# The last 512 positions of a down projection, by pairs of tiles and partly by seven products for eight

## The chip, the cores and the metric

The kernel runs on one core of a Trainium2 chip. The metric is the device time of one execution in microseconds. Before the change the median of three timed runs is 467.15 us (467.04 to 467.17).

A core has five engines that run side by side and meet at semaphores: TensorE (PE; its weight loads are listed apart as PEld), VectorE (DVE), ScalarE (ACT), GpSimd (POOL) and SyncE (SP), from which all DMA transfers of this kernel are issued, one after the other.

## The reference

A layer norm over 2048 positions of 512 channels feeds two branches. Branch A is a windowed attention (32 heads, 8 keys each, every second position) with its output weights `wo`. Branch B is two layers with a squared ReLU, then a Silu. The result is the input plus their product.

```python
def _B_ref(x, w1, b1, w2, b2):                 # D = 512, F = 1792
    h = jnp.einsum("bsd,df->bsf", x, w1) + b1
    r = jnp.where(h > 0, h, 0)
    h = r * r
    return jnp.einsum("bsf,fd->bsd", h, w2) + b2

x = A_x                                        # 1 x 2048 x 512
xn = _layernorm(x, axis=-1)
s = _A_ref(xn, A_wqkv, A_wo)                   # attention, then o @ wo
g = _silu(_B_ref(xn, B_w1, B_b1, B_w2, B_b2))
return x + s * g
```

What the change touches is the second einsum, the down projection, for the last quarter of the positions.

## The kernel before

All matrix products are in float32 precision, made of three passes each: an operand is split into a high part that TensorE takes as float32r and a low rest, and a product is high x high, high x low and low x high (`PASSES`). A split costs a copy on ACT and a subtraction on VectorE or GpSimd. The query, key, value and up projections already replace eight products of blocks by seven in large parts, with sums and differences of blocks as operands; the down projection does not.

The down projection is tiled into chunks of `C` = 512 positions (`NCH` = 4), each of four tiles of 128 positions (`TPC` = 4). It runs over `NF` = 14 blocks f of 128 of the 1792 inner channels. `down(c, f, j)` gives three matmuls of 512 columns into the bank `pbs[c, j]`, with 128 positions of `h` standing in the array and the rows of w2 moving. `begin` writes the bias b2 into a bank before; `gate` takes Silu out of it afterwards. The four banks have the tag "acc", of which there are four.

`h` is made from the up projection's result `u`, which for chunks 2 and 3 is loaded from the memory `su` by `load_ut`, six blocks ahead, into a ring of 12 pieces of 2 KB per partition (the tag "z" of the pool `keep`). `make_h`, two blocks ahead, squares it on ACT (with a ReLU first for half of the blocks), once into the high part and once in place, and an E instruction takes the difference as low part. Two blocks share a buffer of the tag "h", of which there are two.

Beside this, VectorE works through the attention in eight units of 256 positions. Its results are stored to `so`, loaded by `load_o` in another order, transposed by `trans_o` on VectorE, split (ACT, then `lowo`), and multiplied by `wo` in `out_product`: 12 matmuls of 512 columns a tile. `finish` multiplies this by the gate, adds x and stores the tile. In chunk 3 the out products of tiles 8 and 9 stand ahead of its first block, those of 10 and 11 after f = 5 and f = 6, those of 12 and 13 before the last three blocks; then each tile does its last three blocks and its gate, and the out products of tiles 14 and 15 end the kernel, the last one in two halves of 256 columns.

The order of work on each engine is not that of the program. `Book` records every instruction, plans the whole kernel by prices and due times, and then fixes the order on each engine. Only TensorE keeps the program's order. Instructions given to `E` go to VectorE or GpSimd, as the plan chooses. Every instruction is issued by one helper, so all have the same line in the profile (L163), and the names of tiles tell them apart: `pb` is a bank of the down projection, `pw` of an out product, `ut` and `h` its inputs, `z` a gated tile, `v`, `pv`, `Lp` are attention, `oq`, `oTf`, `oT` its outputs on the way to the out product, `pv` on TensorE a bank of the value projection.

Of the kernel before, what the change touches and what calls it, by code (L numbers as in the profile page):

```python
# [55 lines left out]
HOME2 = (Q0, T2, T3, K1, T4, V0, V1)  # L56

CUT = (Q0, T2, T3, T4, V1)

WARM = 20  # L60
WARM2 = 1
# [505 lines left out]
def trace(ctx: ExitStack, tc: tile.TileContext, plan, x, wqkv, wo, w1, b1, w2, b2, out):  # L567
# [37 lines left out]
    def split(hi, lo, src, eng):  # L605
        high(hi, lo, src)
        low(hi, lo, src, eng)
# [252 lines left out]
    def load_w2(f):  # L860
        w2raws[f] = piece(f"w2r{f}")
        dma(w2raws[f], w2[f * P:(f + 1) * P, :])
# [637 lines left out]
    def load_ut(c, f):  # L1500
        uts[c, f] = keep.tile([P, 2, 256], F32, name=f"ut{c}_{f}", tag="z", bufs=12)
        n = 256 * (c % 2)
        dma(uts[c, f], su[f][:, :, n:n + 256])

    def make_h(c, f):
        if (c, f) == (0, 0):
            h = hs[c, f] = [wts.tile([P, 512], FR, name=f"h{c}_{f}_{i}", tag=f"s{i}") for i in (T4, V1)]
        else:
            if f % 2 == 0 or (c, f) == (0, 1):
                hpair[f // 2] = p2.tile([P, 2, 2, 512], FR, name=f"h{c}_{f}", tag="h", bufs=2)  # L1510
            h = hs[c, f] = [hpair[f // 2][:, f % 2, i] for i in range(2)]
        n = 256 * (c % 2)
        if c >= NCH // 2:
            parts = [(uts.pop((c, f)).rearrange("p e n -> p (e n)"), h)]
        elif f < 4:
            parts = [(u0[f, e][:, n:n + 256], [x[:, e * 256:(e + 1) * 256] for x in h]) for e in range(2)]
        else:
            parts = [(u0[f // 2][f % 2][:, :, n:n + 256], [x.rearrange("p (e n) -> p e n", e=2) for x in h])]
        for u, (hi, lo) in parts:
            if f % 2:  # L1520
                A.activation(u, u, AF.Relu)
            A.activation(hi, u, AF.Square)
            A.activation(u, u, AF.Square)
            E.tensor_sub(lo, u, hi.bitcast(F32))
# [14 lines left out]
    def begin(c, j):  # L1539

        pbs[c, j] = psA(f"pb{c}_{j}")
        A.activation(pbs[c, j], b2t, AF.Copy)

    def down(c, f, j):
        h, w, n = hs[c, f], w2s[f], (j % 2) * 256 + j // 2 * P
        for k, (a, b) in enumerate(PASSES):
            PE.matmul(pbs[c, j], h[a][:, n:n + P], w(f % 2, b), start=False, stop=f == NF - 1 and k == 2,
                      skip_group_check=True)

    oqs, oTs = {}, {}  # L1550

    def load_o(u):
# [40 lines left out]
    def finish(t, eng, xt=None, cols=slice(0, D)):  # L1593
        z = gs[t // TPC, t % TPC]
        if xt is None:
            xt = xrs.pop(t)
        V.tensor_mul(z[:, cols], z[:, cols], pws[t][:, cols])
        eng.tensor_add(z[:, cols], z[:, cols], xt[:, cols])
        dma(tile_rows(out, t)[:, cols], z[:, cols])
# [10 lines left out]
    def split_wo(i):  # L1610
        for g in range(2):
            split(wot[:, 0, 2 * i + g], wot[:, 1, 2 * i + g], rwo[i][:, g], E)

    sequence = [(c, f) for c in range(NCH) for f in range(NF)]

    def ahead_h(c, f):
        i = c * NF + f
        if i + 6 < len(sequence) and i + 6 >= NCH // 2 * NF:
            load_ut(*sequence[i + 6])
        if i + 2 < len(sequence):  # L1620
            make_h(*sequence[i + 2])

    for j in range(TPC):
        begin(0, j)
    make_h(0, 1)
    for c in range(NCH):
        last = c == NCH - 1
        t0 = c * TPC
        for f in range(NF):
            if c == 0 and f in (2, 3):  # L1630
                load_wo(f - 2)
            if c == 0 and f < 8:
                load_w2(f + 6)
                split_w2(f + 6)
            if c == 0 and f in (5, 7):
                split_wo((f - 5) // 2)
            if c:
                if f < 2:
                    finish(t0 - 4 + f, E)
                if f == 2:  # L1640
                    load_o(c * 2 - 1)
                    load_r(t0 - 2)
                    load_r(t0 - 1)
                elif f == 4:
                    trans_o(t0 - 2)
                    trans_o(t0 - 1)
                elif f == 5:
                    lowo(t0 - 2)
                    lowo(t0 - 1)
                elif f == 6:  # L1650
                    out_product(t0 - 2, psT(f"pw{t0 - 2}"))
                elif f == 7:
                    finish(t0 - 2, E)
                    out_product(t0 - 1, psT(f"pw{t0 - 1}"))
                elif f == 8:
                    finish(t0 - 1, E)
            if f >= 7:
                load_o(c * 2)
            if f in (9, 10) and not last:
                load_r(t0 + f - 9)  # L1660
            if f == 11:
                for i in range(2):
                    trans_o(t0 + i)
            if f == 12:
                for i in range(2):
                    lowo(t0 + i)
                load_o(c * 2 + 1)
            ahead_h(c, f)
            if f == 0 and c == 0:
                pass  # L1670
            elif c == 0 and f == 1:
                for i in range(2):
                    for j in range(TPC):
                        down(c, i, j)
            elif f < (NF - 3 if last else NF - 2):
                for j in range(TPC):
                    down(c, f, j)
        if not last:
            for j in range(TPC):
                for i in (2, 1):  # L1680
                    down(c, NF - i, j)
                gate(c, j)
                begin(c + 1, j)
            for i in range(2):
                out_product(t0 + i, psT(f"pw{t0 + i}"))
        else:
            for i in range(2):
                out_product(t0 + i, psT(f"pw{t0 + i}"))
            for i in range(2, TPC):
                trans_o(t0 + i)  # L1690
            for i in range(2, TPC):
                lowo(t0 + i)
            xl = []
            for h in range(2):
                t = four(f"xlast{h}", [2, 512])
                r0 = t0 * P + h * UP
                dma(t.rearrange("p e n -> p (e n)"), x[r0:r0 + UP, :].rearrange("(p e) n -> p (e n)", e=2))
                xl += [t[:, e] for e in range(2)]
            for j in range(TPC):
                for f in range(NF - 3, NF):  # L1700
                    down(c, f, j)
                gate(c, j)
                if j < 2:
                    finish(t0 + j, V, xl[j])
            for j in range(2, TPC):
                n = D // 2 if j == TPC - 1 else D
                for i in range(0, D, n):
                    cols = slice(i, i + n)
                    out_product(t0 + j, (psL if i else psT)(f"pw{t0 + j}_{i}"), cols)
                    finish(t0 + j, V, xl[j], cols)  # L1710

    return book.arrange()

# [21 lines left out]
```

## Time and profile before

| what | value |
|---|---|
| median of three timed runs | 467.15 us |
| the profiled execution | 466.68 us |
| its span | 464.9 us |
| TensorE busy | 458.6 us (99%) |
| VectorE busy | 411.0 us (88%) |
| ScalarE busy | 309.9 us (67%) |
| GpSimd busy | 296.7 us (64%) |
| granted clock of TensorE | 1.0 |

The span goes from the first to the last instruction that the profiler recorded; the time of an execution holds a little more. A group of instructions is listed with its names (out<-in), its shapes, its count, the summed time, the mean duration of one, and the idle time ahead of it with what ended that. Matmuls overlap in the pipeline, so that the mean duration of one (some 390 ns) is longer than its pace; the pace is read from the chain or from start times. Some matmul records are missing from the trace.

### The profile page before, as it was taken

The numbers are of one execution on the slowest core, as the hardware profiler recorded it, in microseconds if no ns is written. First come the engines' busy times: TensorE is split into PE (matmuls) and PEld (weight loads), VectorE is DVE, ScalarE is ACT, GpSimd is POOL, SyncE is SP. The second block draws the span as 40 slices with busy tenths as digits, with TensorE's granted clock in tenths as the row PEclk, the third lists the DMA queues.
The fourth block names the chain that finished last, engine by engine and source line by source line (L and its number), as shares of the span: only waits on it lengthen the run. The fifth ranks groups of instructions, "written<-read, shape, count | busy, mean of one in ns | idle before, by whom it ended". The sixth has DMA issues, their size and how long they took to land.

```text
span 464.9 us, 6411 instructions
## 1 busy us (share of the span) xinstructions
PE 458.6 (99%) x2109; PEld 380.9 (82%) x2109; DVE 411.0 (88%) x349; ACT 309.9 (67%) x589; POOL 296.7 (64%) x309
## 2 busy tenths in 40 slices
PE   8999999999999999999999999999999999999996
PEld 5788888888888888888888888888888888888885
DVE  5984579989999999999999999998999999999432
ACT  5757889956664748477585798796449635953440
POOL 2286438745999899956461699786636655556440
PEclk9999999999999999999999999999999999999999
DMA  7799889899987997475264488597665697541302
GB/s 275 218 249 260 258 260 243 201 299 266 234 230 243 236 274 211 149 208 130 69 170 108 135 254 199 133 256 243 164 154 134 198 229 205 158 139 43 115 0 91
DMA packets 72589, 88.83 MB, mean 191 GB/s; under 512 B 6764, under 2 KB 52076, under 8 KB 72556
## 3 DMA queue, kind: packets, MB, share of 16 engines
q1 hardware_dynamic: 72556, 88.43, 69.9%
q8 instruction: 16, 0.26, 0.2%
q14 instruction: 17, 0.14, 0.1%
HBM read 54.80 MB, written 30.47 MB: 183 GB/s over the span
## 4 chain that ended last, share of the span: by engine, by line
PE 96%; DMA 1%; DVE 1%; ACT 0%; SPq 0%; issue 0%
PE pb L163 33%; PE uX L163 16%; PE pm L163 12%; PE pw L163 9%; PE uZ L163 8%; PE pq L163 8%; PE pv L163 4%; PE uY L163 4%; DMA wqraw<-in_A_wqkv 1%; SPq L163 0%; DVE wq L163 0%; PE pxT L163 0%; DVE z L163 0%; ACT wq L163 0%; DVE st L163 0%
## 5 line engine op out<-in xcount | busy, mean ns | idle before, releaser
L163 PE MATMUL pb<-w,h 128*128 128x512 f32 x592 | 149.2, 390 | 0.0
L163 PEld LDWEIGHTS pb<-w,h 128*128 128x128 f32 x592 | 110.9, 188 | 23.5 <-POOL h L163 0.4
L163 DVE TENSOR_TENSOR pr<-k,qp 128x2048 f32<-128x2048 f32 x32 | 72.8, 2274 | 2.4 <-ACT qp L163 1.8
L163 DVE TENSOR_TENSOR pv<-v,Lp 128x2048 f32<-128x2048 f32 x32 | 73.0, 2283 | 0.7
L163 DVE TENSOR_REDUCE v<-pv 128x256 f32<-128x2048 f32 x32 | 72.9, 2279 | 0.5
L163 DVE TENSOR_REDUCE L<-pr 128x128 f32<-128x2048 f32 x32 | 72.8, 2276 | 0.4
L163 POOL TENSOR_TENSOR h<-ut,h 128x512 fp32r<-128x512 f32 x25 | 32.2, 1301 | 28.6 <-ACT ut L163 28.6
L163 PE MATMUL pw<-wot,oT 128*128 128x512 f32 (+1 forms) x204 | 45.5, 377 | 0.0
L163 POOL TENSOR_TENSOR h<-u,h 128x256 fp32r<-128x256 f32 (+1 forms) x30 | 30.6, 1035 | 22.8 <-ACT u L163 21.2
L163 PEld LDWEIGHTS pw<-wot,oT 128*128 128x128 f32 x204 | 36.8, 188 | 7.1
L163 ACT ACTIVATE h<-ut 128x512 fp32r<-128x512 f32 x28 | 16.4, 627 | 21.9 <-PE pb L163 12.2
L163 ACT ACTIVATE ut<-ut 128x512 f32<-128x512 f32 x42 | 24.7, 626 | 9.3 <-DMA ut<-su 9.3
L163 POOL TENSOR_TENSOR u<-u,more 128x512 f32<-128x512 f32 x14 | 18.1, 1301 | 19.6 <-ACT more L163 19.2
L163 ACT ACTIVATE u<-uX,b1t 128x512 f32<-128x512 f32 x28 | 19.2, 684 | 15.5 <-PE uX L163 15.3
L163 POOL TENSOR_TENSOR oT<-oTf,oT 128x512 fp32r<-128x512 f32 x16 | 25.5, 1601 | 3.3 <-ACT oT L163 3.3
L163 ACT ACTIVATE u<-u 128x512 f32<-128x512 f32 (+1 forms) x54 | 26.1, 527 | 0.1
L163 ACT ACTIVATE oT<-oTf 128x512 fp32r<-128x512 f32 x16 | 18.2, 1139 | 11.5 <-DVE oTf L163 6.7
L163 ACT ACTIVATE h<-u 128x512 fp32r<-128x512 f32 (+1 forms) x36 | 17.5, 529 | 10.5 <-PE pb L163 10.4
L163 DVE TENSOR_TENSOR z<-z,pw 128x512 f32<-128x512 f32 (+1 forms) x17 | 11.1, 650 | 12.2 <-ACT z L163 7.3
L163 ACT ACTIVATE stg<-pm 128x512 f32<-128x512 f32 x30 | 17.7, 599 | 5.8 <-PE pm L163 5.6
L163 PE MATMUL pq<-wq,XA 128*128 128x512 f32 x78 | 20.2, 392 | 0.3 <-DVE wq L163 0.3
L163 PE MATMUL uZ<-SA,w1s 128*128 128x512 f32 x84 | 20.2, 390 | 0.0
(193 smaller groups left out, 1049.5 us busy)
## 6 DMA issues: line engine op xcount, KB each, us to landing
k<-sk SPq DMA_DIRECT2D x8, 960.0 KB, 7.6
v<-sv SPq DMA_DIRECT2D x8, 960.0 KB, 7.4
su<-u SPq DMA_DIRECT2D x28, 256.0 KB, 3.3
ut<-su SPq DMA_DIRECT2D x28, 256.0 KB, 3.8
x<-in_A_x SPq DMA_DIRECT2D x16, 256.0 KB, 4.6
sk<-stg SPq DMA_DIRECT2D x8, 512.0 KB, 4.0
sq<-stg SPq DMA_DIRECT2D x8, 512.0 KB, 3.7
sv<-stg SPq DMA_DIRECT2D x8, 512.0 KB, 3.5
```

What stands on the lines that cost most here:

```text
L163: ins = f(*a, **k)
```

## The change

Chunks 0 to 2 stay as they are. Chunk 3 is done by two pairs p of tiles (12 and 13, then 14 and 15), each in seven steps s. A step takes the blocks f = s and s + 7 for both tiles of the pair. Its operands are a 2 x 2 arrangement of blocks (two tiles, two f) against a 2 x 2 arrangement (two f, the left and right 256 columns of w2).

A plain step is 12 matmuls of 512 columns into banks 0 and 1. A step of seven (`SEVENTHS`: the last three of pair 0, the last five of pair 1) is seven products of three passes with 256 columns, spread over four banks, with sums of blocks as operands:

- `sum_w2`, during chunk 2, loads the two blocks of w2 again for s = 2 to 6, forms four sums of 256 columns, and splits them.
- `make_step` makes, beside the squares of a plain step, four sums of 128 columns of `h` and splits these too. The buffers come from the tag "h", or, for one step at a time, from the attention's "v" (`place_h`; `fill` makes steps as far as buffers allow).
- `join` copies the four banks of a pair out and adds their quarters up with seven additions, then takes Silu.

The out products of tiles 8 to 13 move between the steps (`jobs`); those of 14 and 15 follow the last `join`.

```diff
+DSEVEN = range(2, 7)
+SEVENTHS = range(4, 7), DSEVEN
+WHOME = {2: "m", 3: "m", 4: f"b{T1}", 5: f"b{K0}", 6: f"b{Q1}"}
...
+    def sum_w2(s):
+        for f in (s, s + NF // 2):
+            load_w2(f)
+        a, b = (w2raws.pop(f) for f in (s, s + NF // 2))
+        lo, hi = slice(0, 256), slice(256, 512)
+        E.tensor_sub(a[:, lo], a[:, hi], a[:, lo])
+        E.tensor_sub(a[:, hi], b[:, hi], a[:, hi])
+        E.tensor_sub(b[:, hi], b[:, hi], a[:, lo])
+        E.tensor_sub(b[:, lo], b[:, lo], b[:, hi])
...
+        for i, r in enumerate((a, b)):
+            split(t[i][:, 0], t[i][:, 1], r, E)
+        wsum[s] = t
...
+    def place_h(p, s):
+        if s in SEVENTHS[p]:
+            tag = "h" if live["v"] else "v"
+            live[tag].append((p, s))
+            if tag == "v":
+                return att.tile([P, 2, 7, P], FR, name=f"hs{p}_{s}", tag="v")
+            return p2.tile([P, 2, 7, P], FR, name=f"hs{p}_{s}", tag="h", bufs=2)
+        if s % 2 == 0:
+            cuts[p] = p2.tile([P, 2, 2, 4, P], FR, name=f"hs{p}_{s}", tag="h", bufs=2)
+            live["h"].append((p, s + 1))
+        return cuts[p][:, s % 2]
...
+    def make_step(p, s):
+        u = uts.pop((p, "s", s)).rearrange("p (q n) -> p q n", n=P)
...
+        A.activation(part, part, AF.Relu)
+        n = 3 if s in SEVENTHS[p] else 4
+        A.activation(h[:, 0, :n], u[:, :n], AF.Square)
+        A.activation(u, u, AF.Square)
+        E.tensor_sub(h[:, 1, :n], u[:, :n], h[:, 0, :n].bitcast(F32))
+        if s in SEVENTHS[p]:
+            f = piece(f"fs{p}_{s}").rearrange("p (q n) -> p q n", n=P)
+            E.tensor_add(f[:, 0], u[:, 3], u[:, 2])
+            E.tensor_sub(f[:, 1], f[:, 0], u[:, 0])
+            E.tensor_sub(f[:, 2], u[:, 0], u[:, 3])
+            E.tensor_sub(f[:, 3], u[:, 1], f[:, 1])
+            A.activation(h[:, 0, 3:], f, AF.Copy)
+            E.tensor_sub(h[:, 1, 3:], f, h[:, 0, 3:].bitcast(F32))
...
+    def begin_pair(p):
+        banks[p] = [psA(f"pd{p}_{i}") for i in range(4)]
+        for i in range(2):
+            A.activation(banks[p][i], b2t, AF.Copy)
+
+    def step(p, s):
...
+        for bank, half, q, r, cols in ((0, lo, 1, v[1], lo), (1, lo, 2, t[1], lo), (2, lo, 0, v[0], lo),
+                                       (3, lo, 3, t[0], lo), (3, hi, 5, t[0], hi), (2, hi, 4, t[1], hi),
+                                       (0, hi, 6, v[1], hi)):
+            for k, (a, c) in enumerate(PASSES):
+                PE.matmul(b[bank][:, half], h[:, a, q], r(c)[:, cols],
...
+    def join(p):
...
+        for t, b in zip((za, zb, x, y), banks.pop(p)):
+            A.activation(t, b, AF.Copy)
+        E.tensor_add(x[:, hi], x[:, hi], x[:, lo])
+        E.tensor_add(za, za, x)
+        E.tensor_add(za[:, hi], za[:, hi], y[:, lo])
+        E.tensor_add(x[:, hi], x[:, hi], y[:, hi])
+        E.tensor_add(zb[:, lo], zb[:, lo], x[:, hi])
+        E.tensor_add(x[:, hi], x[:, hi], y[:, lo])
+        E.tensor_add(zb[:, hi], zb[:, hi], x[:, hi])
+        for e, z in enumerate((za, zb)):
+            A.activation(z, z, AF.Silu)
+            gs[NCH - 1, 2 * p + e] = z
...
+            if c == NCH - 2 and f % 2 == 0 and f // 2 < len(DSEVEN):
+                sum_w2(DSEVEN[f // 2])
...
+    jobs = {(0, 0): [(leave, t0 - 4)], (0, 1): [(leave, t0 - 3), (oT_of, t0 // 2 - 1), (rows_of, t0 // 2 - 1)],
+            (0, 3): [(leave, t0 - 2)], (0, 5): [(leave, t0 - 1), (oT_of, t0 // 2), (rows_of, t0 // 2)],
+            (0, 6): [(join, 0), (leave, t0), (begin_pair, 1)],
+            (1, 3): [(leave, t0 + 1), (oT_of, t0 // 2 + 1), (rows_of, t0 // 2 + 1)],
+            (1, 6): [(join, 1)]}
+    for p in range(2):
+        for s in range(NF // 2):
+            i = n * NF + p * (NF // 2) + s
+            step(p, s)
+            if i + 6 < len(sequence):
+                load_step(sequence[i + 6][0], sequence[i + 6][2])
+            for f, a in jobs.get((p, s), ()):
+                f(a)
+            fill((p, s))
+    for t in range(t0 + 2, NT):
+        leave(t, True)
```

`leave` is the out product and the finish of a tile, `oT_of` the load, transposition and split of two tiles' attention outputs, `rows_of` the load of two tiles of x. `load_step` loads the `u` of a step in two transfers of 128 KB with runs of 512 bytes, where `load_ut` had one of 256 KB with runs of 1 KB.

More of the change, by code (lines that the diff above doesn't have):

```diff
@@ L1548, in down @@
                       skip_group_check=True)
+    wsum, steps, cuts = {}, {}, {}
+    def sum_w2(s):
[7 more added lines that the diff above has]
+        E.tensor_sub(b[:, lo], b[:, lo], b[:, hi])
+        if WHOME[s] == "m":
+            t = [four(f"w2s{s}_{i}", [2, 512], FR) for i in range(2)]
+        else:
+            t = wts.tile([P, 2, 2, 512], FR, name=f"w2s{s}", tag=WHOME[s])
+            t = [t[:, i] for i in range(2)]
+        for i, r in enumerate((a, b)):
+            split(t[i][:, 0], t[i][:, 1], r, E)
+        wsum[s] = t
@@ new lines, in load_step @@
+    def load_step(p, s):
+        t = uts[p, "s", s] = piece(f"us{p}_{s}")
+        t = t.rearrange("p (q n) -> p q n", n=P)
+        n = 256 * ((NCH - 1) % 2) + P * p
+        for i in range(2):
+            dma(bass.AP(tensor=t.tensor, offset=t[:, i].offset, ap=[t.ap[0], [(3 - 2 * i) * P, 2], [1, P]]),
+                su[s + i * (NF // 2)][:, :, n:n + P])
+    live = {"h": [], "v": []}
+    def place_h(p, s):
[9 more added lines that the diff above has]
+        return cuts[p][:, s % 2]
@@ new lines, in fill @@
+    def fill(at):
+        for tag in live:
+            live[tag] = [o for o in live[tag] if o > at]
+        while made:
+            p, s = made[0]
+            if len(live["h"]) == 2 and (s % 2 == 0 if s not in SEVENTHS[p] else live["v"]):
+                return
+            made.pop(0)
+            make_step(p, s)
+    def make_step(p, s):
+        u = uts.pop((p, "s", s)).rearrange("p (q n) -> p q n", n=P)
+        h = place_h(p, s)
+        steps[p, s] = h
+        i = 1 - s % 2
+        part = bass.AP(tensor=u.tensor, offset=u[:, i].offset, ap=[u.ap[0], [(3 - 2 * i) * P, 2], [1, P]])
+        A.activation(part, part, AF.Relu)
[11 more added lines that the diff above has]
+            E.tensor_sub(h[:, 1, 3:], f, h[:, 0, 3:].bitcast(F32))
@@ new lines, in trace @@
+    banks = {}
+    def begin_pair(p):
+        banks[p] = [psA(f"pd{p}_{i}") for i in range(4)]
+        for i in range(2):
+            A.activation(banks[p][i], b2t, AF.Copy)
+    def step(p, s):
+        h, b = steps.pop((p, s)), banks[p]
+        fs = (s, s + NF // 2)
+        if s not in SEVENTHS[p]:
+            for i, f in enumerate(fs):
+                for e, q in ((0, i), (1, 3 - i)):
+                    for a, c in PASSES:
+                        PE.matmul(b[e], h[:, a, q], w2s[f](f % 2, c), start=False, stop=False, skip_group_check=True)
+            return
+        lo, hi = slice(0, 256), slice(256, 512)
+        w, v = wsum[s], [lambda c, f=f: w2s[f](f % 2, c) for f in fs]
+        t = [lambda c, i=i: w[i][:, c] for i in range(2)]
+        for bank, half, q, r, cols in ((0, lo, 1, v[1], lo), (1, lo, 2, t[1], lo), (2, lo, 0, v[0], lo),
[3 more added lines that the diff above has]
+                PE.matmul(b[bank][:, half], h[:, a, q], r(c)[:, cols],
+                          start=s == SEVENTHS[p][0] and bank > 1 and half == lo and k == 0,
+                          stop=s == DSEVEN[-1] and k == 2, skip_group_check=True)
@@ new lines, in join @@
+    def join(p):
+        za, zb = (p2.tile([P, D], F32, name=f"z{NCH - 1}_{2 * p + e}", tag="z", bufs=5) for e in range(2))
+        x, y = piece(f"x16{p}"), piece(f"x57{p}")
+        lo, hi = slice(0, 256), slice(256, 512)
+        for t, b in zip((za, zb, x, y), banks.pop(p)):
[10 more added lines that the diff above has]
+            gs[NCH - 1, 2 * p + e] = z
@@ L1595, in finish @@
         if xt is None:
-            xt = xrs.pop(t)
+            xt = xrs[t]
         V.tensor_mul(z[:, cols], z[:, cols], pws[t][:, cols])
@@ L1612, in split_wo, with ahead_h @@
             split(wot[:, 0, 2 * i + g], wot[:, 1, 2 * i + g], rwo[i][:, g], E)
[L1614 to L1621, printed above, removed]
+    sequence = [(c, f) for c in range(NCH - 1) for f in range(NF)] + [(p, "s", s) for p in range(2) for s in range(NF // 2)]
+    def ahead_h(i):
+        if i + 6 < len(sequence):
+            n = sequence[i + 6]
+            if len(n) == 3:
+                load_step(n[0], n[2])
+            elif n[0] >= NCH // 2:
+                load_ut(*n)
+        i += 2
+        if i < len(sequence):
+            n = sequence[i]
+            if len(n) == 2:
+                make_h(*n)
+    made = [(p, s) for p in range(2) for s in range(NF // 2)]
     for j in range(TPC):
@@ L1625, in trace @@
     make_h(0, 1)
-    for c in range(NCH):
-        last = c == NCH - 1
+    for c in range(NCH - 1):
         t0 = c * TPC
@@ L1658, in trace @@
                 load_o(c * 2)
-            if f in (9, 10) and not last:
+            if f in (9, 10):
                 load_r(t0 + f - 9)
@@ L1667, in trace @@
                 load_o(c * 2 + 1)
-            ahead_h(c, f)
+            ahead_h(c * NF + f)
             if f == 0 and c == 0:
@@ L1674, in trace @@
                         down(c, i, j)
-            elif f < (NF - 3 if last else NF - 2):
+            elif f < NF - 2:
                 for j in range(TPC):
                     down(c, f, j)
[L1678 to L1682, printed above, removed]
+        more = c < NCH - 2
+        if not more:
+            live["h"].append((-1, 0))
+            fill((-2, 0))
+        for j in range(TPC):
+            for i in (2, 1):
+                down(c, NF - i, j)
+            gate(c, j)
+            if more:
@@ L1683, in trace @@
                 begin(c + 1, j)
+        if more:
             for i in range(2):
                 out_product(t0 + i, psT(f"pw{t0 + i}"))
[L1686 to L1710, printed above, removed]
@@ new lines, in leave, with oT_of, rows_of @@
+    def leave(t, last=False):
+        if t < NT - 1:
+            out_product(t, psT(f"pw{t}"))
+            return finish(t, V if last else E)
+        for i in range(0, D, D // 2):
+            cols = slice(i, i + D // 2)
+            out_product(t, (psL if i else psT)(f"pw{t}_{i}"), cols)
+            finish(t, V, None, cols)
+    def oT_of(u):
+        load_o(u)
+        for i in range(2):
+            trans_o(2 * u + i)
+        for i in range(2):
+            lowo(2 * u + i)
+    def rows_of(u):
+        for i in range(2):
+            load_r(2 * u + i)
@@ new lines, in trace @@
+    n = NCH - 1
+    t0 = n * TPC
+    begin_pair(0)
+    fill((-1, 0))
+    jobs = {(0, 0): [(leave, t0 - 4)], (0, 1): [(leave, t0 - 3), (oT_of, t0 // 2 - 1), (rows_of, t0 // 2 - 1)],
[7 more added lines that the diff above has]
+            step(p, s)
+            if i + 6 < len(sequence):
+                load_step(sequence[i + 6][0], sequence[i + 6][2])
+            for f, a in jobs.get((p, s), ()):
+                f(a)
+            fill((p, s))
```

## The prediction

> **What bounds the kernel now.** First the page, for who is busy; then the chain that ended last, which gives the pace of each kind of product and the tail; then busy time by stretches and the order in time of single engines around the place that is rebuilt.
>
> ```profile
> span 464.9 us, 6411 instructions
> PE 458.6 (99%) x2109; PEld 380.9 (82%) x2109; DVE 411.0 (88%) x349; ACT 309.9 (67%) x589; POOL 296.7 (64%) x309
> 20.61 21.79 PE pq L163 x96
> 80.04 1.44 PE pv L163 x12
> 406.20 16.32 PE pb L163 x72
> 430.68 10.88 PE pb L163 x48
> 455.16 5.60 PE pw L163 x36
> 460.76 0.03 issue
> 460.79 0.43 DVE z L163
> ```
>
> The kernel is bound by TensorE. From 20.61 to 460.76 us the chain is matmuls back to back (in it "pieces" give start, length, what, count). So a product taken out saves its pace, unless something else becomes late. After the last product come a multiplication, an addition and a store: 464.9 - 460.76 = 4.1 us. The profiled execution took 466.68 us, 1.78 us more than its span; the median of the three timed runs is 467.15. I work on the profiled execution and add the difference of 0.47 at the end.
>
> **The products.** A 512-column product paces at 16.32 / 72 = 226.7 ns, a 256-column one at 1.44 / 12 = 120 ns. The last piece agrees: 36 products, 12 of 512 (2.72) and 24 of 256, leave 2.88 / 24 = 120 ns. A plain step has 2 x 2 x 3 = 12 products of 512 columns, 2.72 us, as many as one of today's f has. A step of seven has 7 x 3 = 21 products of 256, 2.52 us. Each saves 0.20 us and eight save **1.6 us**. Everything else on TensorE stays in number: six plain steps, eight out products, the last in halves. From below: the step saves nothing from 2.72 / 21 = 130 ns a product on, and both rows stand at 120; from above, the shortest pieces (0.71 us for six) give 118.3 ns, 0.236 a step and 1.9 us in all.
>
> The Trainium skill ("TensorE: Matmul & The Clock Gate", Back-to-back issue gap) gives N / 2.4 + 2.5 ns for a product alone, 215.7 and 109.2 ns for 512 and 256 columns; by it the saving would be 0.295 a step and 2.4 us in all. The rows above show 226.7 and 120 ns, so the measured paces decide.
>
> **The tail.** Today the gates of the last tiles run beside out products, and only the last half tile waits.
>
> ```profile
> 455.00 5.75 PE L163 MATMUL pw<-wot,oT 128*128 128x512 f32 x36
> 455.25 0.60 ACT L163 ACTIVATE z<-pb 128x512 f32<-128x512 f32 x1 [1.49 <-PE pb L163]
> 457.98 0.69 DVE L163 TENSOR_TENSOR z<-z,pw 128x512 f32<-128x512 f32 x1 [4.33 <-issue]
> 458.70 0.69 DVE L163 TENSOR_TENSOR z<-z,xlast 128x512 f32<-128x512 f32 x1
> 459.41 0.42 DVE L163 TENSOR_TENSOR z<-z,pw 128x256 f32<-128x256 f32 x1
> 459.86 0.42 DVE L163 TENSOR_TENSOR z<-z,xlast 128x256 f32<-128x256 f32 x1
> 460.79 0.42 DVE L163 TENSOR_TENSOR z<-z,pw 128x256 f32<-128x256 f32 x1 [0.50 <-PE pw L163]
> 461.25 0.42 DVE L163 TENSOR_TENSOR z<-z,xlast 128x256 f32<-128x256 f32 x1
> ```
>
> The two last out products (tiles 14 and 15) start at T = 455.00, and the last addition ends at T + 6.67. Afterwards, what stands between the last step and them is `join(1)`: four copies on ACT, seven additions, two Silu, and then the same products and finishes. The copies are mostly early, since banks 1, 3 and 2 are complete 15, 6 and 3 products (1.8, 0.7, 0.4 us) before T. ACT starts 0.25 after a product and paces at about 0.54 a copy, so bank 2 is out at T + 0.7, bank 0 at T + 1.2. The additions form one chain: six of 256 columns at 0.45 from start to start and one of 512 at 0.72, from T + 0.7 with 0.1 of waiting to T + 4.2. The Silu of tile 15 ends near T + 4.8, while TensorE is still at the out products until T + 5.6. But VectorE also has tile 14's multiplication and addition (1.4) and tile 15's four halves (1.8): 4.2 + 1.4 + 1.8 = T + 7.4. So VectorE ends the tail, not TensorE: +0.75, less some 0.15 where neighbours don't depend on each other (two of 512 columns took 1.28 together). I take **+0.6**. Lower end 0: GpSimd takes an addition and the end is TensorE's again. Upper end 1.5 (a rival below). No table of ACT is loaded there if Silu's is in since `join(0)`.
>
> **The buffer of the fifth step.** The first two steps' `h` take the buffer that f = 10 and 11 of chunk 2 leave, the next two that of f = 12 and 13. The fifth, (0, 4), is the first of seven, and it is written into the attention buffer "v", free only when the last `v` that used it (rows of positions 1536 to 1791) is stored.
>
> ```profile
> 400.60 5.60 PE L163 MATMUL pw<-wot,oT 128*128 128x512 f32 x24
> 406.64 0.68 DVE L163 TENSOR_TENSOR z<-z,pw 128x512 f32<-128x512 f32 x1
> 409.44 0.68 DVE L163 TENSOR_TENSOR z<-z,pw 128x512 f32<-128x512 f32 x1
> 410.03 2.28 DVE L163 TENSOR_REDUCE v<-pv 128x256 f32<-128x2048 f32 x1
> 412.47 0.56 SPq L163 DMA_DIRECT2D so<-v  x1
> 416.31 1.72 SPq L163 DMA_DIRECT2D oq<-so  x4
> 442.44 1.31 DVE L163 STREAM_TRANSPOSE oTf<-oq 128x512 f32<-128x512 f32 x2 [6.50 <-DMA oq<-so]
> ```
>
> Chunk 2's down products end at 400.60. Four plain steps and the out products of tiles 8, 9 and 10 are 7 x 2.72 = 19.04 us, so TensorE comes to (0, 4) at 419.64; its fourth product of seven, the first that needs the sums, comes nine matmuls on, at 420.7. Today the last reduction into that `v` ends at 412.3 and its store is done by 416.3, when the load of what it wrote is issued.
>
> ```profile
> L163 POOL TENSOR_TENSOR h<-ut,h 128x512 fp32r<-128x512 f32 x25 | 32.2, 1301 | 28.6 <-ACT ut L163 28.6
> L163 POOL TENSOR_TENSOR w1r<-w1r,w1r 128x256 f32<-128x256 f32 x20 | 15.2, 768 | 0.4
> L163 DVE TENSOR_TENSOR h<-ut,h 128x512 fp32r<-128x512 f32 x3 | 2.1, 684 | 0.6 <-ACT ut L163 0.6
> L163 DVE TENSOR_TENSOR h<-u,h 128x512 fp32r<-128x512 f32 x5 | 6.4, 1283 | 0.0
> L163 ACT ACTIVATE h<-ut 128x512 fp32r<-128x512 f32 x28 | 16.4, 627 | 21.9 <-PE pb L163 12.2 <-issue 9.7
> L163 ACT ACTIVATE u<-u 128x256 f32<-128x256 f32 x24 | 8.9, 412 | 0.1
> ```
>
> From the free buffer to the first sum in `h`: a square of 384 columns, 0.52 (between 412 and 627 ns), one of 512, 0.54 behind it, four additions of 128 columns on GpSimd (estimate 0.49 each with their gap, from 768 for 256 columns and 1301 for 512), the copy 0.6, the low part 1.30, and some 0.7 of hand-overs: 5.6 us. With today's 416.3 this gives 421.9, **1.2 us late**. But tile 9's out product now ends near 411.5, so its multiplication (0.6 of VectorE) can't stand ahead of that reduction any more, and tile 8's needn't: the buffer is free at 415.1 to 415.7, late by 0 to 0.6. VectorE can also do the low part in 0.68 instead of 1.30. I take **+0.4**, with 0 as the lower end; the upper end is the rival below. No later step is as tight: by the same count (0, 5) and (0, 6) have 13 and 10 us from the buffer to the use, and the last three steps 7.7.
>
> **What else is added, and its cover.**
>
> ```profile
> ut<-su SPq DMA_DIRECT2D x28, 256.0 KB, 3.8
> w2r<-in_B_w SPq DMA_DIRECT2D x14, 256.0 KB, 3.1
> 445.00:461.00 16.00, 15.75 (x81) 13.34 (x79) 5.02 (x9) 4.14 (x6) 2.43 (x2) 1.00 0.13 49
> 452.36 1.28 DVE L163 TENSOR_TENSOR z<-z,xlast 128x512 f32<-128x512 f32 x2
> ```
>
> Ten more loads of w2 rows, and 28 loads of 128 KB in place of 14 of 256 KB, go through SP's one queue, at some 0.5 us an issue and in runs half as long. They land in 3 to 4 us and are issued six steps (16 us) ahead: nothing, with 12 us of cover; were that gone, a step would wait for its landing. Between the pairs ACT has six copies (3.3 us) of which the first starts 1.5 us before the last product, against 2.72 us of out product 12: nothing. At the start of pair 0 no out products stand ahead of the first step.
>
> ```profile
> 397.11 1.28 ACT L163 ACT_TABLE_LOAD   x1
> 398.41 1.09 ACT L163 ACTIVATE z<-pb 128x512 f32<-128x512 f32 x2
> 399.38 1.12 ACT L163 ACTIVATE pb<-b2t 128x512 f32<-128x512 f32 x2
> ```
>
> The first two banks would be filled at 399.99 and 400.50, needed at 400.60 and 401.28: nothing, at worst 0.5. Attention's last output reaches VectorE at 442.44 and the out product of tile 14 starts near 453.4, so a few microseconds of VectorE time after 412 are free.
>
> The sum: -1.6 + 0.6 + 0.4 = **-0.6**, 466.1 for the profiled execution, 466.5 on the median.
>
> **The rivals.** *Full gain*: both added terms are covered, by GpSimd taking an addition of the tail and by squares and sums that find the buffer at 415.1. Time 467.15 - 1.6 = 465.55, to 465.3 at the shorter pace. For it: GpSimd has 2.43 us of work in the last 16 (the fifth engine of the row above). Against: the additions are one chain, and most of it is VectorE's own work.
>
> *GpSimd runs over, and the fifth step waits* (slower). The sums of w2 need, for each of five steps, four subtractions of 256 columns and two low parts of 512: 4 x 0.768 + 2 x 1.30 = 5.7 us on GpSimd, 28.4 in all, most of it before (0, 4).
>
> ```profile
> 340.00:352.00 12.00, 12.00 (x55) 9.94 (x54) 11.93 (x9) 7.75 (x14) 3.85 (x3) 1.00 0.68 165
> 401.00:412.00 11.00, 11.00 (x50) 9.09 (x50) 10.93 (x7) 8.92 (x16) 8.00 (x6) 1.00 0.42 123
> sum 72.00, PE 72.00 PEld 59.62 DVE 71.65 ACT 47.96 POOL 40.49; mean PE 12.00 PEld 9.94 DVE 11.94 ACT 7.99 POOL 6.75
> ```
>
> Between 340 and 412 GpSimd (last of the five engines in a row) has 72 - 40.5 = 31.5 us free, VectorE 0.35. It just fits, if nothing else comes; each step of seven itself adds some 3 us. What doesn't fit goes to VectorE, ahead of the reduction that frees the buffer: 7 of the 28 us would be some 3 us there, and the wait of 0.4 becomes 3. Time 467.15 - 1.6 + 0.6 + 3 = 469.1. Against: the w2 pieces can be loaded as soon as their ring has room, the sums for (1, 2) and (1, 3) are used late, and VectorE has slack after 412. It decides from a wait of 1.9 us, a buffer free later than 417.0; today it is 416.3.
>
> *VectorE and GpSimd block each other in the tail.* The same subtraction took 684 ns on VectorE for three, 1283 for five others that stood beside GpSimd's work. If the join's additions are spread over both engines, two of them cost 0.6 more each: tail +1.5 rather than 0.6, time 467.4. The Trainium skill ("SBUF — State Buffer", Who interferes with whom) says that a VectorE instruction with two SBUF inputs contends with a GpSimd one that reads SBUF; the 1283 agrees.
>
> That the change doesn't do what it says would be a 256-column pace of 130 ns: the rows exclude it.
>
> **How the numbers follow.** My forecast 0.40; full gain 0.24; GpSimd runs over 0.26; blocked tail 0.10. A measurement of this kernel tells about 0.2%, 0.93 us, from no change. The forecast (466.0 to 467.0 by its two terms) splits 0.10 faster, 0.30 the same; the full gain is faster; running over is slower but for 0.02; the blocked tail the same. Faster 0.34, the same 0.42, slower 0.24. The range, 465.4 to 468.8, leaves out the upper half of running over (0.13) and a little below.
>
> **What would show it.** Each step of seven 2.5 us long and no gap of TensorE but one before (0, 4), under 1 us, with its releaser ACT or GpSimd on `hs`; the store of `v` issued near 411.5; VectorE without a gap from T + 0.7 to the end, its last addition near T + 7.3. Wrong: gaps at other steps (sums of w2 late, bias copies at the start of the pair), a store of `v` after 414, or a pace of 256-column products other than 120 ns.

## The result and the profile after

The changed kernel takes **473.77 us** (median of four runs, 468.31 to 474.97) against 467.10 us before on the same chip: ratio 1.0121, 95% interval 1.0082 to 1.0159. It is slower by 1.2%; the forecast was 466.5, the range 465.4 to 468.8. The profiled execution took 473.61 us, 6.93 more than that of before (466.68). One of the four runs took only 468.31 us, at a granted clock of 1.00 (0.990 to 0.995 in the others); no trace of it is kept, but the early loss told of below seems not to come in every execution. Ratios leave out runs of over 1.5% above the fastest of their kernel, which three_sums alone has (two of four).

From the page of the changed kernel, its span, its busy time and the granted clock in 40 slices:

```profile
span 471.8 us, 6722 instructions
...
PE 460.0 (97%) x2181; PEld 384.9 (82%) x2181; DVE 429.3 (91%) x366; ACT 325.0 (69%) x622; POOL 347.9 (74%) x376
...
PEclk9999999999979999999999999999999999999998
```

TensorE is busy for 1.4 us more than before (458.6), has gaps now, and its clock falls once ahead of the end, in the twelfth slice (129.7 to 141.5 us). GpSimd has 51 us more work. To see where the time went, the chains of both kernels are compared at the same marks. First before:

```profile
133.18 1.39 PE uZ L163 x6
...
139.39 2.72 PE uY L163 x12
...
400.76 5.44 PE pw L163 x24
```

and after:

```profile
136.66 1.65 PE pv L167 x6
138.31 2.56 PE uZ L167 x6
...
146.14 2.72 PE uY L167 x12
...
409.01 2.72 PE pd L167 x12
...
435.83 2.51 PE pd L167 x21
...
454.31 7.55 PE pd L167 x63
461.86 5.63 PE pw L167 x36
467.93 0.42 DVE z L167
```

| stretch | before | after | change |
|---|---|---|---|
| start to the products `uY` | 139.39 | 146.14 | +6.75 |
| from there to the end of chunk 2 | 261.37 | 262.87 | +1.50 |
| the rebuilt products, to the last out products | 54.40 | 52.85 | -1.55 |
| from there to the end of the last addition | 6.51 | 6.82 | +0.31 |

The four add up to +7.01, the difference between the ends of the last additions (461.67 and 468.68). The rebuilt part gains what was forecast, and nearly the whole loss lies **270 us ahead of it**, in code that the change doesn't touch. TensorE's waits in the changed kernel (total, times, longest):

```profile
PE pv L167 <- ACT stg L167: 4.0, 1, 4.0
...
PE pb L167 <- POOL h L167: 1.2, 1, 1.2
```

The first one, engine by engine in order of time: VectorE, GpSimd, ACT, TensorE.

```profile
128.40 0.68 DVE L167 TENSOR_TENSOR stg<-stg,pm 128x512 f32<-128x512 f32 x1
129.00 6.64 DVE L167 TENSOR_TENSOR stg<-stg,stg 128x512 f32<-128x512 f32 x1
...
129.22 3.82 POOL L167 TENSOR_TENSOR w1s<-w1r,w1s 128x512 fp32r<-128x512 f32 x3
132.96 0.76 POOL L167 TENSOR_TENSOR w1r<-w1r,w1r 128x256 f32<-128x256 f32 x1
133.65 0.76 POOL L167 TENSOR_TENSOR w1b<-w1r,w1b 128x256 fp32r<-128x256 f32 x1
134.33 0.76 POOL L167 TENSOR_TENSOR w1r<-w1r 128x256 f32<-128x256 f32 x1
137.71 1.28 POOL L167 TENSOR_TENSOR w1b<-w1r,w1b 128x512 fp32r<-128x512 f32 x1 [2.62 <-ACT w1b L167]
...
135.73 0.60 ACT L167 ACTIVATE stg<-pm 128x512 f32<-128x512 f32 x1 [5.76 <-DVE stg L167]
...
136.66 1.01 PE L167 MATMUL pv<-wq,SB 128*128 128x256 f32 x3 [4.01 <-ACT stg L167]
```

An addition of 512 columns with both inputs in the SBUF, into a quarter of a key tile, takes 6.64 us on VectorE. The addition ahead of it, with one input from TensorE's bank (`pm`), takes 0.68. GpSimd meanwhile works without a gap until 135.09, and the addition ends 0.55 us after that. ACT's next copy waits for it, and TensorE for ACT. GpSimd itself stops only when its next input must come from ACT, which waits for VectorE.

The clock adds to it. Ten-microsecond windows of the changed kernel (the five engines' busy time, granted clock, DMA share, GB/s):

```profile
120.00:130.00 10.00, 10.00 (x60) 8.81 (x59) 9.93 (x7) 6.98 (x14) 10.00 (x13) 1.00 0.90 213
130.00:140.00 10.00, 5.99 (x26) 4.93 (x25) 10.00 (x4) 2.60 (x6) 7.38 (x9) 0.75 0.70 183
140.00:150.00 10.00, 10.00 (x45) 8.41 (x44) 9.90 (x6) 6.51 (x11) 5.09 (x6) 0.91 0.55 159
```

After the wait six products of 512 columns take 2.56 us (427 ns each; 1.39 us before), and the loss is 6.75 us rather than 4.0. The Trainium skill ("TensorE: Matmul & The Clock Gate", Part 1: The HAM clock gate) says that an idle window of about 3.4 us halves the clock, and gives 426.7 ns for 512 columns then; the row agrees.

Before, the plan had put this addition on GpSimd itself, where it took its turn:

```profile
128.36 1.30 POOL L163 TENSOR_TENSOR stg<-stg,stg 128x512 f32<-128x512 f32 x1
```

`Book` plans the whole kernel at once. The work that the change adds made it choose differently from the start: of the 2933 recorded instructions that both kernels have ahead of the first new one, 22 changed engine, and many their place. `Book` does price the two engines' contention: in its plan (`lock` in `forward`) such an instruction of one starts only when that of the other has ended, in the planned order, so that the addition would wait for one GpSimd instruction at most. In the kernel only the order within each engine is fixed, and the addition waited for the whole row.

### The profile page after: what moved, and what is told of

Its sections match the earlier page's. It is cut to its first block, busy times and chain, and to the rows that moved or that the text cites. A ratio compares the mean times of both kernels' runs of the same rounds, so it can differ in the third digit from the quotient of the medians.

```text
span 471.8 us, 6722 instructions
## 1 busy us (share of the span) xinstructions
PE 460.0 (97%) x2181; PEld 384.9 (82%) x2181; DVE 429.3 (91%) x366; ACT 325.0 (69%) x622; POOL 347.9 (74%) x376
## 4 chain that ended last, share of the span: by engine, by line
PE 65%; POOL 3%; issue 1%; DMA 1%; ACT 0%; SPq 0%; DVE 0%; DVEq 0%; POOLq 0%; ACTq 0%
PE pb L167 21%; PE uX L167 16%; PE uZ L167 8%; PE pw L167 8%; PE pd L167 8%; PE uY L167 4%; DMA us<-su 1%; POOL h L167 1%; POOL w2r L167 1%; PE pv L167 1%; POOL w2s L167 1%; POOL oT L167 0%; POOL z L167 0%; POOL L L167 0%; ACT stg L167 0%
## 5 line engine op out<-in xcount | busy, mean ns | idle before, releaser
L167 PE MATMUL pb<-w,h 128*128 128x512 f32 x444 | 112.1, 390 | 1.2 <-POOL h L167 1.2
L167 PEld LDWEIGHTS pb<-w,h 128*128 128x128 f32 x444 | 83.0, 188 | 19.4 <-POOL h L167 2.0
L167 PE MATMUL pd<-w,hs 128*128 128x512 f32 (+1 forms) x127 | 28.2, 336 | 0.0
L167 POOL TENSOR_TENSOR oT<-oTf,oT 128x512 fp32r<-128x512 f32 x15 | 24.5, 1634 | 4.3 <-ACT oT L167 2.6
L167 PEld LDWEIGHTS pd<-w,hs 128*128 128x128 f32 x127 | 21.8, 189 | 2.7
L167 POOL TENSOR_TENSOR w1s<-w1r,w1s 128x512 fp32r<-128x512 f32 x14 | 18.1, 1312 | 5.5 <-ACT w1s L167 5.4
L167 ACT ACTIVATE us<-us 128x256 f32<-128x256 f32 (+1 forms) x28 | 14.1, 522 | 11.1 <-DMA us<-su 10.9
L167 PE MATMUL uZ<-SA,w1s 128*128 128x512 f32 x84 | 21.4, 406 | 0.0
L167 POOL TENSOR_TENSOR h<-ut,h 128x512 fp32r<-128x512 f32 x13 | 16.7, 1297 | 5.8 <-ACT ut L167 5.7
L167 POOL TENSOR_TENSOR rs<-rs,mhalf 128x1 f32<-128x1 f32 x16 | 10.4, 656 | 14.2 <-DVE rs L167 13.1
```

The costliest lines, as they stand in the source:

```text
L167: ins = f(*a, **k)
```

## The experiments

The theory after the two traces: (a) the 6.75 us are the new plan's, by a VectorE addition that gets no turn at the SBUF while GpSimd works without a gap; (b) the rebuilt products are worth the 1.55; (c) the sums of w2 cost the 1.5 us in chunk 2, by GpSimd's time. Rivals: the early loss is an effect of the new work itself or the addition only runs slower; the moved out products cost time; the waits in chunk 2 are those of loads.

The plan is a list of instructions in order, with an engine (V or G) for each E instruction. It is made from a first trace and used in a second, and between the two it can be edited.

### Whose loss is the early one?

**before_late_order**: the program of before, the start of its plan in the order and on the engines of the changed kernel. **after_early_order**: the reverse. `first` and `engines` are written into the kernel.

```diff
+def early(plan):
...
+    kept, given = set(first), list(plan[1])
+    for n, e in zip(first, engines):
+        given[n] = e
+    order = first + [n for n in plan[0] if n not in kept]
...
-    trace(tc, plan, *aps)
+    trace(tc, early(plan), *aps)
```

> The kernel before, none of the change in it, but its first 2545 instructions (to the first that the change adds) in the order and on the engines that the plan of the kernel after gives them. Theory: the same lock, 473 to 474.5 us, though nothing of the down projection has changed. Rival (the change's own work makes the loss): 467.1.

> The kernel after, but its first 2553 instructions in the order and on the engines of the kernel before. Theory: TensorE runs without a gap to chunk 2; then -1.6 of the products, +0.3 of the tail, +1.4 of the wait in chunk 2 for the low part of h, and up to 0.4 for the fifth step's buffer: 467.0 to 467.7. Rival (rebuilt part): near 473.8.

The kernel of before with the new order took 474.90 us against 467.11 (ratio 1.0171, 1.0132 to 1.0210), with nothing of the change in it. Its trace has the same addition and the same wait:

```profile
129.03 6.62 DVE L163 TENSOR_TENSOR stg<-stg,stg 128x512 f32<-128x512 f32 x1
...
PE pv L163 <- ACT stg L163: 4.0, 1, 4.0
```

So the early loss belongs to the start of the plan alone, its order and its engines. The changed kernel with the old order took 469.67 (ratio 1.0051, 1.0035 to 1.0068): the early loss is gone, but it missed the expected 467.7 by 2 us, since more waits stand in chunks 1 and 2 then. They come back below.

### One addition, or a way of planning?

**one_addition** gives just that addition back to GpSimd; **two_additions** the next one too.

```diff
+    plan[1][1068] = "G"                     # one_addition
+    plan[1][1068] = plan[1][1127] = "G"     # two_additions
     trace(tc, plan, *aps)
```

> The kernel after, its order of work kept, but the one addition stg<-stg,stg of the last pair of projection tiles is given back to GpSimd. Theory (this VectorE instruction with two SBUF inputs waits 6 us behind GpSimd's unbroken row, and TensorE 4.0 us for it): no wait of TensorE at pv, granted clock 1.00 throughout, 466.9 to 467.6 us. Rival (the loss comes from the rebuilt part, and the early gap is hidden anyway): still near 473.8.

> The kernel after, its order kept, with both additions of the last pair (stg<-stg,stg and the first stg<-vtmp,stg) on GpSimd. Theory (each VectorE instruction with two SBUF inputs waits for a gap in GpSimd's row, so that the second was caught when the first was moved): no VectorE addition above 2.5 us near 130 us, no gap of TensorE before chunk 1; what is left is the wait in chunks 1 and 2: 468.0 to 469.7. Rival (something else early in this order holds TensorE up): 471 and more.

one_addition missed: 473.41 us (ratio 1.0132, 1.0105 to 1.0159). The next addition with two inputs in the SBUF was caught instead, behind a row of GpSimd that now ran without a gap until 140.66:

```profile
132.74 8.21 DVE L167 TENSOR_TENSOR stg<-vtmp,stg 128x256 f32<-128x256 f32 x1 [0.49 <-issue]
...
138.53 2.13 POOL L167 TENSOR_TENSOR w1r<-w1r,w1r 128x256 f32<-128x256 f32 x3
```

With both on GpSimd the time is 467.94 us (466.38 to 469.71 in ten runs; ratio 1.0029, 1.0012 to 1.0046), and no wait of TensorE of over 0.3 us is left after the start of the kernel in the profiled run, the fastest. Of the 6.7 us over before, 1.1 is left once two instructions are moved. Why the ten runs spread over 3.3 us isn't settled; the waits of chunk 2 (below) may come and go from run to run.

### Slower work, or no turn?

**short_addition** makes the caught addition 64 columns wide instead of 512; the other sums of that quarter are left out. `SHORT` is set between the two traces, so that the plan is that of the changed kernel.

```diff
-            E.tensor_add(k[:, :, 1], k[:, :, 1], q[:, :, 1])
+            cut = slice(0, 8 if SHORT[0] and a == 14 else CH)
+            E.tensor_add(k[:, :, 1, cut], k[:, :, 1, cut], q[:, :, 1, cut])
```

> The changed kernel, plan and order untouched, with one instruction made short: the VectorE addition into the third quarter of stg that took 6.64 us at 129.0 now adds 64 of its 512 columns (the other sums are left out), which as work alone is about 0.1 us instead of 0.69. Theory that VectorE waits there for a gap in GpSimd's unbroken row (128 to 135): its length is set by that row, so it still takes 5.5 to 6.7 us, TensorE still waits about 4 us for ACT's stg, and the time stays at 472.5 to 474.5. Rival that both engines share the SBUF evenly and the addition is only slowed in proportion to its size: it takes at most 1 us, TensorE's wait is gone, and the time falls to 466.5 to 468.5.

473.36 us (ratio 1.0139, 1.0126 to 1.0152). An eighth of the work takes nearly as long:

```profile
128.94 6.18 DVE L167 TENSOR_TENSOR stg<-stg,stg 128x64 f32<-128x64 f32 x1
...
134.31 0.73 POOL L167 TENSOR_TENSOR w1r<-w1r 128x256 f32<-128x256 f32 x1
```

It ends 0.08 us after GpSimd's row. In the changed kernel and in three_sums and late_four_sums below (512 columns) the addition ends 0.55 to 0.56 us after the last GpSimd instruction of the row, in one_addition (256) 0.29, here (64) 0.08: its whole work, some 1.1 ns a column, is done after the gap has come. For this addition it is **a wait for the gap**, as long as the row.

The Trainium skill ("SBUF — State Buffer", Who interferes with whom) says that a VectorE instruction with two SBUF inputs contends with a GpSimd one that reads the SBUF, and that of two that contend for the shared ports the one issued first holds them for its instruction. The rows agree on who contends; but here VectorE lost to five and more GpSimd instructions in succession, not to one.

Most such instructions are not caught. In the trace of the changed kernel 28 of VectorE's additions and subtractions with two inputs in the SBUF began while GpSimd ran an instruction that the next one followed without a gap. 26 of them ended before that next one did, one outlasted it, and this one outlasted six. An example of the 26 (GpSimd, then VectorE):

```profile
402.40 1.27 POOL L167 TENSOR_TENSOR h<-ut,h 128x512 fp32r<-128x512 f32 x1 [1.73 <-ACT ut L167]
403.63 1.75 POOL L167 TENSOR_TENSOR z<-z,xr 128x512 f32<-128x512 f32 x1
...
402.88 1.34 DVE L167 TENSOR_TENSOR h<-ut,h 128x512 fp32r<-128x512 f32 x1 [2.06 <-ACT ut L167]
```

VectorE ends 0.55 us after the first GpSimd instruction, and now GpSimd seems to be the one that waits: its next one takes 1.75 us, where one of 512 columns takes some 1.3 (1.27 just ahead). In all 14 traces there are 286 such instructions; 278 outlasted at most one further GpSimd instruction, six outlasted 5 to 15 (6.2 to 11.6 us), and two outlasted two and three (2.4 us in three_sums_moved, 3.4 in late_four_moved). What decides which of them is caught stays open.

### What the moved out products and the sums cost

**plain_steps** keeps the old start of the plan and does all 14 steps as plain ones: pairs and moved out products stay, the sums, the four banks and the seven additions go. **narrow_sums** has the old start and all steps of seven, but does the four subtractions for each step's sums of w2 on 8 of 256 columns, in the second trace only (`WIDTH[0]` is 256 in the first and 8 in the second); the rest of those sums is left out.

```diff
-SEVENTHS = range(4, 7), DSEVEN
+SEVENTHS = range(7, 7), range(7, 7)              # plain_steps
...
-        lo, hi = slice(0, 256), slice(256, 512)
+        lo, hi = slice(0, WIDTH[0]), slice(256, 256 + WIDTH[0])     # narrow_sums
```

> As after_early_order, but all 14 steps plain: no step of seven, no sums of w2, no join of four banks (Silu straight from two). If GpSimd's load from the sums makes the wait in chunk 2: no gap of TensorE, 466.8 to 467.4, with 168 products of 512 columns as before. If the new places of the out products make it: a gap of 1.4 stays, 468.5.

> As after_early_order, same order and engines, but the four subtractions of each sum of w2 work on 8 columns in place of 256 (the sums are incomplete): some 12 us less on GpSimd in chunks 1 and 2, all loads and splits as they were. Theory (GpSimd's time makes the waits): TensorE's gaps of 3.5 us in chunks 1 and 2 shrink below 1 us, 466.8 to 467.6. Rival (the ten added loads, or a ReLU that waits in ScalarE's queue for its load, make them): 469.3 to 469.8 as before.

plain_steps: 466.69 us, ratio 0.9992 (0.9983 to 1.0001), no wait of TensorE beyond those of before. The moved out products cost nothing, and the extra waits in chunks 1 and 2 come with the steps of seven: the sums, and the loads and splits for them. How after_early_order spends them, in TensorE's waits, and in windows with GpSimd (the fifth engine) at 9.33 and 29.64 us of 10 and 30, where the kernel before has 5.11 and 19.13:

```profile
PE pb L167 <- POOL h L167: 3.2, 3, 1.7
...
320.00:330.00 10.00, 8.34 (x36) 6.59 (x37) 10.00 (x7) 9.61 (x16) 9.33 (x9) 1.00 0.51 165
360.00:390.00 30.00, 30.00 (x134) 24.82 (x133) 29.83 (x22) 17.93 (x31) 29.64 (x27) 1.00 0.72 202
```

```profile
320.00:330.00 10.00, 10.00 (x46) 8.29 (x45) 7.82 (x6) 6.68 (x10) 5.11 (x4) 1.00 0.57 184
360.00:390.00 30.00, 30.00 (x134) 24.84 (x133) 29.89 (x22) 15.90 (x26) 19.13 (x15) 1.00 0.73 209
```

narrow_sums took 468.61 (ratio 1.0035, 1.0022 to 1.0049), between what the theory and the rival expected: 1.06 us less than after_early_order, some 0.8 by the two ratios. TensorE's waits for `h` are 2.0 us in its trace against 3.2, but the 3.2 are of a run that took 470.75, the longest of the four of after_early_order:

```profile
PE pb L168 <- POOL h L168: 2.0, 5, 0.8
```

The subtractions are 4 x 0.77 = 3.1 of the 5.7 us that a step's sums take of GpSimd. So (c) seems to hold in part: GpSimd's time for the sums makes some of the waits. Another part shows on ACT, whose queue holds a ReLU of a later step, which waits for its load, ahead of the squares of the next block. At the wait of 1.2 us in the changed kernel (ACT, GpSimd, TensorE):

```profile
400.20 0.42 ACT L167 ACTIVATE us<-us 128x256 f32<-128x256 f32 x1 [4.01 <-DMA us<-su]
400.53 1.14 ACT L167 ACTIVATE h<-ut 128x512 fp32r<-128x512 f32 x2
...
402.40 1.27 POOL L167 TENSOR_TENSOR h<-ut,h 128x512 fp32r<-128x512 f32 x1 [1.73 <-ACT ut L167]
...
403.73 0.73 PE L167 MATMUL pb<-w,h 128*128 128x512 f32 x2 [1.20 <-POOL h L167]
```

narrow_sums has the same picture (ACT waits 3.94 us for a load at 395.21). How the waits divide between the splits of the sums, the lateness of these loads and their place in ACT's queue stays open. More pieces for the ring, which would give the loads more lead, were not tried.

### Fewer sums, and at another time

**three_sums**: as after_early_order, with three steps of seven in each pair (two sums less). **late_sums**: pair 0 plain, three steps of seven in pair 1, and the sums made during pair 0's steps instead of chunk 2. **late_four_sums**: four of them.

```diff
-DSEVEN = range(2, 7)
+DSEVEN = range(4, 7)      # three_sums, late_sums; range(3, 7) in late_four_sums
...
-SEVENTHS = range(4, 7), DSEVEN
+SEVENTHS = range(7, 7), DSEVEN      # late_sums, late_four_sums
...
-            if c == NCH - 2 and f % 2 == 0 and f // 2 < len(DSEVEN):
-                sum_w2(DSEVEN[f // 2])
...
     for p in range(2):
         for s in range(NF // 2):
+            if p == 0 and s % 2 == 0 and s // 2 < len(DSEVEN):
+                sum_w2(DSEVEN[s // 2])
```

> As after_early_order, but only three sums of w2 (s = 4 to 6), used by both pairs: six steps of seven rather than eight, 17 us of GpSimd in place of 28. Theory: -1.2 for the products, +0.3 for the tail, 0.5 to 1.5 of waits: 466.7 to 467.7. If the loads and not GpSimd decide: waits of 2 us, 468.2.

> As after_early_order, but pair 0 has plain steps, pair 1 three steps of seven (s = 4 to 6), and their sums of w2 are made during pair 0 rather than in chunk 2. Theory: chunks 1 and 2 run without a gap as in plain_steps (466.7), -0.6 for the products, +0.3 for the join's additions in the tail: 466.2 to 466.8. Rival (the sums hold up pair 0's low parts): 467.5 and more.

> late_sums with a fourth step of seven in the second pair (four steps, four sums, all made during the first pair's steps, none for the first pair). Theory that a sum costs nothing where GpSimd has free time and every step of seven is worth 0.2 us of products: four steps give -0.8, the longer join +0.3: 466.0 to 466.7, no TensorE wait over 0.5 us, and from the first pd to the last pw 53.6 to 53.8 us. Rival that a fourth sum no longer fits in the first pair's steps: TensorE waits for a w2 piece or for h or hs in the second pair, 467 and more.

late_sums came as expected: 466.29 us against 466.85, ratio 0.9990 (0.9980 to 0.9999), without a wait. The other two missed: three_sums took 469.72, 476.19, 477.14 and 477.87 us in its four runs (ratio 1.0129, 1.0048 to 1.0210, from the first two), late_four_sums 470.75 (ratio 1.0082, 1.0068 to 1.0096). Their traces, that of three_sums from the run of 477.14, show the caught addition again, now in the rebuilt part itself, at a low part `hs`. three_sums (VectorE, the last of GpSimd's unbroken row, TensorE):

```profile
436.80 11.61 DVE L167 TENSOR_TENSOR hs<-us,hs 128x512 fp32r<-128x512 f32 x1
...
446.45 1.40 POOL L167 TENSOR_TENSOR z<-z,x 128x256 f32<-128x256 f32 x2
...
448.46 2.50 PE L167 MATMUL pd<-w,hs 128*128 128x512 f32 x5 [7.61 <-DVE hs L167]
```

and late_four_sums (VectorE, the last of GpSimd's row, and two waits of TensorE, for what VectorE did late):

```profile
428.62 7.43 DVE L167 TENSOR_TENSOR hs<-us,hs 128x512 fp32r<-128x512 f32 x1
...
434.17 1.33 POOL L167 TENSOR_TENSOR hs<-us,hs 128x512 fp32r<-128x512 f32 x1
...
449.74 0.50 PE L167 MATMUL pd<-w2s,hs 128*128 128x256 f32 x2 [1.41 <-ACT hs L167]
451.16 1.09 PE L167 MATMUL pd<-w2s,hs 128*128 128x256 f32 x7 [0.92 <-DVE hs L167]
```

In late_four_sums these two waits, with 0.5 us of products between them, were followed by a granted clock of 0.59 (452 to 454 us) and 0.70 (454 to 457): here two short waits close together cost pace as well.

**three_sums_moved** and **late_four_moved** give that one addition to GpSimd.

```diff
+    plan[1][3551] = "G"     # three_sums_moved; plan[1][3458] in late_four_moved
     trace(tc, early(plan), *aps)
```

> three_sums with the one addition of 11.61 us (the low part of hs, on VectorE at 436.8) given to GpSimd, all else as it was. Theory: the wait of 7.6 us in the second pair's products goes, and what is left beside the kernel before is the two waits of chunks 1 and 2 (0.9 and 0.8 us), the six steps of seven (-1.2) and the longer join (+0.3): 466.5 to 467.7, no wait of TensorE over 1.3 us, unless a later addition with two SBUF inputs is caught in its place, which would show as another VectorE TENSOR_TENSOR of over 3 us. Rival that three sums cost the products themselves something: the wait stays at several us with no long addition on VectorE, 470 and more.

> late_four_sums with one instruction moved: the VectorE addition into the low part of hs that took 7.43 us at 428.62, behind GpSimd's row of 424 to 435.5, is GpSimd's own; nothing else differs. Theory that this one addition is all that late_four_sums lost: VectorE's queue no longer stands for 7 us, the waits of TensorE for hs (1.4 and 0.9 us) go, and four steps of seven are worth 0.8 us against 0.3 for the join: 466.0 to 466.8. Rival that four sums and their pieces are themselves too much for the second pair, or that the next addition with two SBUF inputs is caught in the same way: a wait for hs of over 0.8 us stays, 467.3 and more.

three_sums_moved took 468.37 us (467.06 to 470.05 in ten runs; ratio 1.0030, 1.0021 to 1.0040), with one instruction moved. This median is 1.35 to 9.50 us below the four runs of three_sums, and 0.7 above what was expected. In its trace the wait of 7.6 us is gone. TensorE waits 1.2 us for `h`, and its last out products start at 455.90, 0.90 later than before; the last addition ends 7.46 us after that start (6.67 before), where 0.3 more had been allowed. late_four_moved took 466.43 us against 466.73 (ratio 0.9991, 0.9982 to 1.0000), 4.3 us less than without the move, and TensorE has no wait for `hs` left.

late_sums and late_four_moved beat both kernels in their medians, by 0.6 and 0.3 us against before. This lies within the 0.2% that the prediction called no change.

## Why the prediction was wrong

- **The products**: right. The eight steps of seven give 52.85 - 54.40 = -1.55 us (forecast -1.6), 2.51 us a step.
- **The tail**: +0.31 rather than +0.6. "VectorE ends the tail, not TensorE" was wrong: the forecast had all seven additions on VectorE, while GpSimd took two of them, which is the prediction's lower end. VectorE waits for the last product here:

```profile
463.53 0.99 POOL L167 TENSOR_TENSOR z<-z,x 128x256 f32<-128x256 f32 x1 [2.49 <-DVE z L167]
465.39 0.74 POOL L167 TENSOR_TENSOR z<-z,x 128x256 f32<-128x256 f32 x1 [0.88 <-ACT z L167]
...
467.59 0.42 DVE L167 TENSOR_TENSOR z<-z,pw 128x256 f32<-128x256 f32 x1 [0.33 <-PE pw L167]
```

- **The buffer of the fifth step**: 0 rather than +0.4; the step follows its out product without a gap. In two_additions, which has no early loss, the last reduction into that `v` (below) ends 6.7 us after the end of chunk 2 (401.79), against 11.6 in the kernel before (412.31 and 400.76): VectorE came to it earlier, by more than the 1.2 us of the two multiplications that no longer stand ahead of it; where the rest comes from was not followed up.

```profile
406.20 2.29 DVE L167 TENSOR_REDUCE v<-pv 128x256 f32<-128x2048 f32 x1
```

- **"What else is added, and its cover"** was priced at nothing, and the stretch to the end of chunk 2 lost 1.5 us, 1.2 of it in the wait for the low part of `h`. The prediction counted landings (3 to 4 us) against six steps of lead, but not who stands behind a load in ACT's queue. It saw GpSimd's free time between 340 and 412 ("it just fits") and put the trouble at the fifth step; it came in chunk 2, at the low part of `h`.
- **The step that failed** is one that the prediction didn't write down: that all work ahead of the change stays where it was, and so adds nothing to the sum. It added 6.75 us. The prediction argued from the order of before, though the plan is made over the whole kernel, and 51 us more on GpSimd change the choice of engine from the start. before_late_order shows that this alone costs as much as the whole change (7.8 us against 6.7).
- **"VectorE and GpSimd block each other"** was a rival, with the right pair of engines and kind of instruction, at 0.10. Its place (the tail) and its price (two instructions, 0.6 each, from 1283 against 684 ns) were wrong. Those 1283 ns fit a wait for one GpSimd instruction, as in the example above and in most of the 286 cases; the prediction took that for the only price. The six that were caught paid the length of GpSimd's unbroken row: 6.2 to 11.6 us.

## What to carry to other kernels

Before pricing a change in a kernel whose order is planned as a whole, ask what the added load does to the order of the work that isn't changed, and after it compare the two chains at common marks from the start. A VectorE instruction with two SBUF inputs beside a long unbroken row of GpSimd waits for one GpSimd instruction as a rule, but now and then for the whole row, and nothing here tells which. Where TensorE would soon stop for it, put it on GpSimd itself, or take one input from TensorE's bank. Added sums cost nothing where GpSimd has gaps (late_sums), and microseconds where it has none.

## What was not expected of the hardware

VectorE got no turn over 5 to 15 GpSimd instructions that followed one another without a gap, for 6.2, 6.6 (twice), 7.4, 8.2 and 11.6 us in six kernels, while 278 of 286 such instructions in the same traces outlasted at most one. The VectorE addition of 512 columns ahead of it in the changed kernel, with one input from a TensorE bank, took 0.68 us beside the same row. And a wait of TensorE of 4.0 us cost 6.75, as the products ran at half their pace after it.
